# Memory-augmented attention on one core: values and memory reads stay dims-on-partitions until the output product, and the softmax sums are inverted by way of DRAM

## The chip, the core and the metric

The kernel runs on one core of a Trainium2 chip. A core has a matrix engine (TensorE, "PE" in the profile, with its weight loads listed apart as "PEld"), three engines for elementwise work (VectorE "DVE", ScalarE "ACT", GpSimd "POOL") and a sync engine ("SP") whose queue issues most of the DMA transfers here. Each engine takes its instructions in the order of its program and stops at one whose operands aren't ready; whatever stands behind it then waits too. TensorE writes its products into PSUM banks, from which the other engines read.

The metric is the device time of one execution in microseconds (us), lower is better; one execution is also recorded by the hardware profiler, and all profile lines come from such a recording.

## What is computed

Four layers act on x of 2048 tokens by 512 features, 32 heads of 16: a linear attention A, a memory-augmented softmax attention B, and both again. The change is in B:

```python
scale = Dh ** -0.5                       # Dh = 16, L = 512 tokens a segment, N = 4 segments
for s in range(N):
    qs, ks, vs = q[:, :, s], k[:, :, s], v[:, :, s]
    p = _softmax(jnp.einsum("bhqd,bhkd->bhqk", qs, ks) * scale + mask, axis=-1)
    a_dot = jnp.einsum("bhqk,bhkd->bhqd", p, vs)
    pq = phi(qs)                         # phi(t) = t + 1 where t > 0, exp(t) elsewhere
    num = jnp.einsum("bhld,bhde->bhle", pq, M)
    den = jnp.einsum("bhld,bhd->bhl", pq, z)[..., None] + 1e-6
    o = g * (num / den) + (1.0 - g) * a_dot        # g = sigmoid(beta), one number a head
    pk = phi(ks)
    M = M + jnp.einsum("bhld,bhle->bhde", pk, vs)
    z = z + jnp.einsum("bhld->bhd", pk)
# x = x + concat(o) @ wo
```

So each head needs two quotients per token: weighted values over the softmax sum, and the memory's read over its own sum. A sum belongs to a head and a token; it divides 16 numbers.

## The kernel before

**Tiling.** A layer B goes through 4 segments `s` of 512 tokens. The 32 heads are 4 chunks `c` of 8 heads, and a chunk is two head groups of 4 (`hf` 0 and 1), so there are 8 groups `m` a segment and 32 a layer. A group has R = 5 steps. `steps` (L1215) is the loop over all steps `k`. In each it issues, in this order: one logits product with its exponential and masks (`attend`), one step of row maxima for a later group (`maxima`, 9 steps ahead), what was put off from earlier steps, the weighted values of the group before (`weighted`, in steps 0 and 2 of the next group), and then the work named by a table. The tables FIRST, GAPS (the two inner segments), LAST (segment 3 when a layer A follows) and FINAL (segment 3 of the last layer) are written by hand: the cell "4.3 a3 fin out/3" says that in step 3 of group 4 a part of chunk 3's memory work, a `finish` and three quarters of an output product are issued. "q2+" is the Q projection of chunk 2 of the next segment, "~" puts an operation's subtraction off to the next step.

**Order.** Two wrappers fix the order on the engines as it was issued: `held` (L173) chains all matmuls, and `Ordered` (L153) chains the instructions of VectorE, ScalarE, GpSimd and SP each among themselves. That is why nearly all lines of the profile are L163 (`Ordered`'s call), L185 (`mm`) and L189 (`tp`, a transpose on TensorE); what an instruction belongs to is seen by its tiles.

**A group's way.** `attend` (L1084) makes logits with keys on partitions into the one double bank `lg`, and ScalarE's exponential reads them into a `P4` tile of 128 x 1024 (`P` in the profile); a row of the operands carries the negated row maxima, so no subtraction is needed. In every step GpSimd zeroes what the causal mask leaves out (`affine_select`, one or two instructions). `weighted` (L1120) multiplies these tiles with the values: the 4 heads of a group stand on 4 column tiles of 32, so the bank `pv` holds, for each head, 16 dims, the softmax sum (a column of ones stands in the values tile `v`, VW = 17 columns a head) and unused rows, with the 512 tokens along the free axis. ScalarE evicts it to `U`, scaled by 1 - g in the dims' rows (`share`).

**Division.** The sum now lies on one partition and the dims that it divides on 16 others. `finish` (L1147), 8 steps (FINAT) after a group's first, turns `U` with four transposes into a `g` bank, tokens on partitions; there `weigh` (L480) takes the reciprocal of the sums on VectorE, multiplies, and adds on GpSimd into the chunk's tile, `ot` (6 buffers) or `tmp` (2), which the memory's read has filled before.

**Memory.** `memory` (L991) reads for segments 1 to 3: four plain f32 products of 128 x 136 a chunk, tokens on partitions, from the features `phi` of Q and the gated state `kn`; `weigh` divides with 1e-6 added. For segments 0 to 2 it updates: four transposes of phi(K), a ScalarE copy, four accumulating f32 products 128 x 136 with the values, an add to `acc`, and two GpSimd multiplies which make `kn` (block diagonal, dims times the gate). `phi` comes from `proj` (L961): ScalarE takes Exp and Relu of the projection, GpSimd takes the minimum with 1 and adds, 128 x 512 each (tiles `tb` in the profile). I call these two GpSimd operations the feature pair.

**Output.** For a segment's four token tiles `turns` (L1156) transposes the four `ot` tiles back (dims on partitions), splits them into a high and a low half (`turn`, L451: ScalarE copies `oh`, VectorE subtracts `ol`), and asks for the residual rows; `out_proj` (L470) makes the product with `wo` in 12 f32r products of 128 x 512 a token tile and adds the residual. `early`, `end_turn` and `end` do this for the last segment of a layer: the product over three chunks early, the fourth at the end.

**Transfers.** SP's queue is one of the ordered programs. It carries, among others, the weight tiles `wqk` for coming projections (512 KB each, asked for in `proj` once a buffer is free) and the stacking of Q and K parts into the tiles `e` that the logits use (`stack`, 128 KB each, issued for the group three ahead).

Of the kernel before, what the change touches and what calls it, by code (L numbers as in the profile page):

```python
# [15 lines left out]
D = 512  # L16
H = 32
# [10 lines left out]
OT = 6  # L28
TA = 8
OO = 3  # L30
# [23 lines left out]
0.4 v3             | 1.1 max m0 q3/2   | 1.3 fin q3~       | 1.4 t1 k3/1  # L54
2.1 max m1 k3      | 2.3 fin ln~       | 2.4 ln~ ln~
3.3 fin q0+/2      | 3.0 w
3.1 max ln~        | 3.4 q0+~ t2
4.1 max k0+/2 load | 4.3 fin k0+/1     | 4.4 k0+ m2
5.0 n              | 5.3 fin q1+/2 n
5.1 max v0+        | 5.4 q1+~ t3  # L60
6.1 max a0+ v1+    | 6.2 n             | 6.3 a0+ fin k1+/2
6.4 k1+ m3         | 7.0 n             | 7.2 n
7.1 max q2+~       | 7.3 fin v2+/2 n   | 7.4 v2+ t0+
# [6 lines left out]
2.1 max a2 m1 k3~  | 2.3 fin ln out/3  | 2.4 out turn~ ln  # L70
3.1 max ln ln out~ | 3.3 a2 fin q0+/2  | 3.4 q0+~ t2
4.1 max k0+~ a3 turn~ load | 4.3 a3 fin out/3 | 4.4 out~ m2
5.0 n              | 5.3 fin v0+/2 n N
5.1 max q1+~ begin | 5.4 v0+ t3
6.0 N              | 6.1 max a0+ k1+~  | 6.2 n
6.3 a0+ fin v1+/3 N | 6.4 v1+ m3       | 7.0 n N
7.1 max q2+~       | 7.2 n N           | 7.3 fin v2+/2 n N
7.4 v2+ t0+
# [3 lines left out]
0.1 max a1 k2~     | 0.2 n             | 0.3 a1 fin v3/3 n  # L82
1.0 n              | 0.4 v3 turn~      | 1.2 n
1.1 max q3~        | 1.3 fin out/2     | 1.4 out turn~
2.1 max k3~        | 2.3 fin a2 out/2  | 2.4 out a2 turn~
3.1 max ln~ ln~    | 3.3 fin out/2 ln~ | 3.4 out ln~ turn~
4.1 max v/2        | 4.3 fin out/2     | 4.4 out v
5.1 max v/2        | 5.3 fin v         | 5.4 a3 pre
6.1 max v/2        | 6.3 fin v a3      | 6.4 v/2 pt~
7.1 p v pt~        | 7.3 fin v/2 p pt  | 7.4 v p pt  # L90
"""
FINAL = """
0.1 max k2~        | 0.3 fin v3/3      | 0.4 v3 a1
1.1 max a1 q3/2    | 1.3 fin q3~       | 1.4 turn~
2.1 max k3/2       | 2.3 fin k3        | 2.4 out/2
3.1 max a2 out turn~ | 3.3 fin out/2   | 3.4 out~ a2
4.1 max a3 turn~   | 4.3 fin out/2     | 4.4 out/1 a3
5.1 max out turn~  | 5.3 fin out/2     | 5.4 out/1 pre
6.1 max out~       | 6.3 fin           | 6.4 pt~
7.1 p pt~          | 7.3 fin p pt      | 7.4 p pt  # L100
# [7 lines left out]
def interleave_kernel(ctx, tc, x_in, a_wqkv, a_wphi, a_wo, b_wq, b_wk, b_wv, b_wo, b_beta,  # L108
# [86 lines left out]
    bd = cp.tile([P, 27], F32, name="bd")  # L195
    bdA, bdB = bd[:, 0:8], bd[:, 8:16]
# [3 lines left out]
    share = cp.tile([P, 8], F32, name="share")  # L200
    ones = cp.tile([32, P], F32, name="ones")

    def constants():
# [11 lines left out]
        dve.tensor_scalar(share, share, -1.0, bd[:, 24:25], op0=ADD, op1=MUL)  # L215
        dve.tensor_scalar(share, share, 1.0, None, op0=ADD)
        dve.tensor_copy(ones, bd[0:32, 25:26].broadcast_to([32, P]))
# [85 lines left out]
    def prepare():  # L303
# [8 lines left out]
        def rows():  # L312

            while jobs and len(asked) < 5:
                src, kc = jobs.pop(0)
                asked.append(T2("ot", OT))
                sync.dma_start(out=asked[-1], in_=src[kc * P : (kc + 1) * P, :])
            return asked.pop(0)
# [4 lines left out]
        def pieces():  # L323
# [10 lines left out]
            for key in ("awo", "bwv", "bwo"):  # L334
                kept[key] = [dtile((P, NC, D), nm(key)) for _ in range(2)]
                for kc in range(NC):
                    tiles = parts()
                    yield tiles, [k[:, kc, :] for k in kept[key]], tiles[1:]
# [141 lines left out]
    def weigh(out, p, eps, add, eng=pool):  # L480
# [914 lines left out]
```

## Time and profile before

| | us |
|---|---|
| three timed runs | 1470.85, 1476.73, 1477.60 |
| their median | 1476.73 |
| the profiled execution | 1472.48 |
| its span, first to last instruction | 1470.8 |
| TensorE busy | 1425.6 |
| VectorE busy | 1089.4 |
| ScalarE busy | 785.5 |
| GpSimd busy | 651.3 |

The granted TensorE clock of the execution was 0.999 of full speed. A row of the groups view reads: line, engine, operation, tile written <- tiles read, partitions x elements, count | busy us, mean ns of one | idle us of the engine just before them, and what ended most of that idle time. PE rows with a form such as 128\*32 tell the tile of the array (rows \* columns). A row of the stretches view gives a window of the span in us, its length, then for PE, PEld, DVE, ACT, POOL and SP's queue the busy us with the number of instructions, then the granted clock, the busy share of the DMA engines and GB/s. A row of the timeline gives start, length in us, engine, line, operation and tiles. A row of the waits view gives engine and tile waiting <- engine and tile waited for, then total us, how often, and the mean.

### The profile page before, as it was taken

How to read it: one execution, taken by the hardware profiler on the slowest of the kernel's cores; microseconds unless marked ns; L12 is line 12 of the kernel's file. 1: busy time of each engine (PE TensorE's matmuls, PEld its weight loads, DVE VectorE, ACT ScalarE, POOL GpSimd, SP SyncE). 2: the span in 40 equal slices, each digit the busy share in tenths (PEclk: the TensorE clock that was granted, in tenths of full speed). 3: DMA queues.
4: the chain of work that ended last, by engine and by line, in shares of the span. 5: the costliest groups of instructions: out<-in, count | busy, mean ns of one | idle time of the engine just before them, and what ended most of it. 6: DMA issues, size and time to landing. Idle time of an engine off the chain costs nothing.

```text
span 1470.8 us, 32374 instructions
## 1 busy us (share of the span) xinstructions
PE 1425.6 (97%) x11908; PEld 1016.5 (69%) x11908; DVE 1089.4 (74%) x3256; ACT 785.5 (53%) x1178; POOL 651.3 (44%) x1000
## 2 busy tenths in 40 slices
PE   7999999999999999999999999999999999999997
PEld 6877778765666666666578887886566666666564
DVE  4766787778877877878656777867777787777883
ACT  5545345446565565566544434543656655655553
POOL 1668654224443544433324456631444454534331
PEclk9999999999999999999999999999999999999999
DMA  5388275546334434544340105754553353343330
GB/s 189 116 301 280 73 258 172 159 125 178 111 104 135 124 95 113 147 102 135 113 160 28 58 30 183 222 185 116 137 166 104 111 148 102 94 133 101 88 99 37
DMA packets 108781, 195.98 MB, mean 133 GB/s; under 512 B 14416, under 2 KB 27856, under 8 KB 107856
## 3 DMA queue, kind: packets, MB, share of 16 engines
q1 hardware_dynamic: 107472, 193.38, 44.0%
q8 instruction: 96, 1.57, 0.4%
q10 hardware_dynamic: 1152, 0.52, 0.1%
q14 instruction: 61, 0.50, 0.1%
HBM read 101.05 MB, written 39.85 MB: 96 GB/s over the span
## 4 chain that ended last, share of the span: by engine, by line
PE 83%; DVE 11%; ACT 3%; issue 2%; DMA 1%; POOL 1%; SPq 0%; POOLq 0%; ACTq 0%; DVEq 0%
PE g L185 49%; PE pv L185 9%; PE lg L185 9%; PE g L189 6%; PE mx L185 5%; PE my L185 3%; DVE mx L163 2%; DVE es L163 1%; DVE my L163 1%; PE lg L189 1%; ACT P L163 1%; DVE mxs L163 1%; DVE tmp L163 1%; DVE ol L163 1%; DVE rr L163 1%
## 5 line engine op out<-in xcount | busy, mean ns | idle before, releaser
L163 ACT ACTIVATE P<-lg 128x1024 f32<-128x1024 f32 x320 | 329.2, 1029 | 174.9 <-PE lg L185 165.5
L163 POOL TENSOR_SCALAR_AFFINE_SELECT P<-P 128x256 f32<-128x256 f32 (+1 forms) x448 | 191.2, 441 | 450.3 <-ACT P L163 449.5
L163 DVE CUSTOM_DVE_ANT_0 mx<-mx,mask 128x128 f32<-128x128 f32 (+3 forms) x512 | 255.3, 499 | 151.7 <-PE my L185 111.2
L163 DVE CUSTOM_DVE_ANT_0 my<-my,mask 128x128 f32<-128x128 f32 (+3 forms) x512 | 265.8, 519 | 6.5
L185 PE MATMUL g<-hh,wqk 128*128 128x512 f32 x512 | 180.2, 406 | 0.7 <-ACT mt L163 0.7
L185 PE MATMUL lg<-e,e 64*128 64x256 f32 (+2 forms) x1024 | 168.5, 387 | 2.8 <-ACT P L163 2.7
L185 PE MATMUL g<-w,oh 128*128 128x512 f32 x512 | 169.5, 412 | 1.0 <-ACT oh L163 0.7
L185 PE MATMUL pv<-P,v 128*32 128x512 f32 (+3 forms) x2048 | 165.0, 441 | 0.0
L185 PE MATMUL my<-e,e 63*128 63x256 f32 (+2 forms) x512 | 146.5, 346 | 6.7 <-DVE mxs L163 5.6
L185 PEld LDWEIGHTS lg<-e,e 64*128 64x128 f32 x1024 | 81.1, 184 | 98.0 <-issue 52.7
L185 PE MATMUL g<-w,hh 128*128 128x512 f32 x448 | 145.7, 406 | 0.1
L163 DVE DVE_READ_ACCUMULATOR2_ANT mxs<- 128x1 f32 x1024 | 144.7, 141 | 0.0
L185 PE MATMUL mx<-e,e 63*128 63x256 f32 (+2 forms) x512 | 140.3, 329 | 0.3
L185 PEld LDWEIGHTS pv<-P,v 128*32 128x32 f32 x2048 | 53.8, 109 | 100.8 <-issue 91.3
L185 PEld LDWEIGHTS g<-hh,wqk 128*128 128x128 f32 x512 | 96.3, 188 | 22.0 <-ACT mt L163 1.1
L185 PEld LDWEIGHTS g<-w,oh 128*128 128x128 f32 x512 | 88.8, 189 | 23.3 <-issue 2.7
L185 PE MATMUL g<-w,ol 128*128 128x512 f32 x256 | 102.4, 400 | 0.0
L185 PE MATMUL g<-hl,wqk 128*128 128x512 f32 x256 | 100.1, 391 | 0.0
L163 ACT CAST ta<-g 128x512 fp32r<-128x512 f32 x64 | 37.6, 587 | 116.0 <-PE g L185 115.7
L185 PEld LDWEIGHTS my<-e,e 63*128 63x128 f32 x512 | 82.2, 185 | 20.4 <-DVE mxs L163 9.2
L185 PEld LDWEIGHTS mx<-e,e 63*128 63x128 f32 x512 | 90.0, 186 | 5.9 <-DVE mxs L163 1.8
L163 POOL TENSOR_SCALAR tb<-tb 128x512 f32<-128x512 f32 x48 | 71.5, 1489 | 49.8 <-ACT tb L163 49.0
(155 smaller groups left out, 2773.6 us busy)
## 6 DMA issues: line engine op xcount, KB each, us to landing
e<-ta SPq DMA_DIRECT2D x384, 128.0 KB
wqk<-wqk SPq DMA_DIRECT2D x64, 512.0 KB
x<-x SPq DMA_DIRECT2D x48, 256.0 KB
ot<-in SPq DMA_DIRECT2D x28, 256.0 KB
pq<-tb SPq DMA_DIRECT2D x24, 256.0 KB
tb<-pq SPq DMA_DIRECT2D x24, 256.0 KB
x<-xr SPq DMA_DIRECT2D x24, 256.0 KB
xr<-x SPq DMA_DIRECT2D x24, 256.0 KB
```

The lines of the kernel that those rows point to most:

```text
L163: i = f(*a, **k)
L185: return held(nc.tensor.matmul(*a, **k))
L189: return held(nc.tensor.transpose(*a))
```

## The change

In layer B the weighted values are no longer turned to tokens on partitions and back. Dims stay on partitions from `pv` to the output product, and so does the memory's read.

- **Values layout.** `v_tile(paired=True)` interleaves two heads, 34 columns a pair, with ones on both sides, so that group hf 0 has its dims on even rows of `pv`, hf 1 on odd ones; `share` is made to match, and the columns of wv are permuted when they are split.
- **After `weighted`.** `gather` takes every second row of `U` into the chunk's tile `tmp` by an SP transfer (hf 0 to rows 0 to 63, hf 1 to 64 to 127), and the sums' four rows into a DRAM tile `den`. For hf 1, `close` schedules the rest at later steps, counted from k = 5(m + 1) + 2.
- **Inversion.** `invert`: `den` in DRAM to a compact tile `dn` of 128 partitions (k + 2), its reciprocal on VectorE (k + 3), out to DRAM `inv` and from there to DRAM `wide`, 16-fold (k + 4), and as tiles of 128 x 512 into `KN` (values) and `mmq` (memory) (k + 5). For segment 0 only the values' half exists.
- **Closing.** At k + 6 GpSimd multiplies `tmp` by its inverse, and for s > 0 `ot` by its own; at k + 7 it adds the two (s > 0), ScalarE copies the result to `oh`, and GpSimd subtracts for `ol`.
- **Read.** Two products of 64 rows, 68 x 512, into `pv` and a `g` bank; two ScalarE evictions, to `ot` and `mmq`, with 1e-6 added to the sums' rows; SP transfers of the sums to `den` (k + 1) and of the upper numerators into `ot` (k + 2).
- **Update.** `tokens` makes the transposes of phi(K) as before; `update` issues 16 products of 32 columns by 34 on four column tiles instead of four of 136, directly behind `weighted`.
- **Output.** `product` uses `oh`, `ol` as they are; `ask` asks for the residual rows. Chunks 2 and 3 of each layer's last segment keep `finish` with its transposes, then `end_turn`; their memory read alone goes through `invert`.
- **Tables and buffers.** `fin` stays only for the last groups and `turn` is gone; `a`, `m` and `t` cells move, `x` cells ask for residual rows; the scheduled pieces are issued at the end of their step. `ot` has 3 buffers instead of 6, `oh` and `ol` 5 instead of 3.

```diff
-OT = 6
+OT = 3
-OO = 3
+OO = 5
...
 GAPS = """
-0.2 n              | 0.3 a1 fin v3/3 n
-0.1 max a1 k2~     | 0.4 v3 turn~ m0
-1.0 n              | 1.2 n
-1.1 max q3~        | 1.3 fin out/2     | 1.4 out t1 turn~
+0.2 n              | 0.3 v3/3 n
+0.1 max k2~        | 0.4 a1 v3 x0
+1.0 m0 n           | 1.2 n
+1.1 max q3~        | 1.3 out/2         | 1.4 t1 out/1 x1
...
+        def at(self, k, f, *a):
+            self.events.setdefault(k, []).append((f, a))
...
+        def read(self, s, c, k):
+            kn, ph = self.summed(s, c)[1], self.st[s, c]["phi", 0]
+            pn = [PS("pv", PV), PS("g", G)]
+            for a in range(2):
+                mm(pn[a][0:68, :], lhsT=kn[64 * a : 64 * a + 64, :], rhs=ph[64 * a : 64 * a + 64, :],
+                   start=True, stop=True, tile_position=(64 * a, 0))
+            old = self.old[s, c] = T2("ot", OT)
+            upper = T2("mmq", 2)
+            for t, p in zip((old, upper), pn):
+                act.activation(t[0:68, :], p[0:68, :], AF.Identity, bias=bd[0:68, 26:27])
+            def dens():
+                d = self.den(s, c)
+                for a, t in enumerate((upper, old)):
+                    sync.dma_start(out=d[12 - 4 * a : 16 - 4 * a], in_=t[64:68, :])
+            def numerators():
+                sync.dma_start(out=old[64:128, :], in_=upper[0:64, :])
+            self.at(k + 1, dens)
+            self.at(k + 2, numerators)
...
+        def invert(self, s, c, k, parts):
+            lo, hi = 8 * parts[0], 8 * parts[-1] + 8
+            n = (hi - lo) * 4
+            tiles = {}
+            def compact():
+                d = tiles["d"] = T2("dn", 2, shape=(P, 64))
+                sync.dma_start(out=d[:, 0:n], in_=self.den(s, c)[lo:hi].rearrange("h (x i) -> (h x) i", i=n))
+            def flip():
+                dve.reciprocal(tiles["d"][:, 0:n], tiles["d"][:, 0:n])
+            def spread():
+                inv, wide = dtile((hi - lo, D), nm("inv")), dtile((hi - lo, DH, D), nm("wide"))
+                sync.dma_start(out=inv.rearrange("h (x i) -> (h x) i", i=n), in_=tiles["d"][:, 0:n])
+                sync.dma_start(out=wide, in_=inv.unsqueeze(1).broadcast_to([hi - lo, DH, D]))
+                tiles["w"] = wide
+            def load():
+                for i in parts:
+                    t = self.inv[s, c, i] = T2(*(("mmq", 2) if i else ("KN", 1)))
+                    sync.dma_start(out=t, in_=tiles["w"][8 * i - lo : 8 * i - lo + 8].rearrange("h d n -> (h d) n"))
+            for j, f in enumerate((compact, flip, spread, load)):
+                self.at(k + j, f)
+        def gather(self, s, c, hf, U):
+            if hf == 0:
+                self.num[s, c] = T2("tmp", 2)
+            sync.dma_start(out=self.num[s, c][64 * hf : 64 * hf + 64, :], in_=U[1 - hf : P : 2])
+            sync.dma_start(out=self.den(s, c)[4 * hf : 4 * hf + 4], in_=U[31 * hf : P : 32])
...
+        def close(self, s, c, k):
+            self.invert(s, c, k + 2, range(2 if s > 0 else 1))
+            def scaled():
+                o = self.num[s, c]
+                pool.tensor_tensor(out=o, in0=o, in1=self.inv.pop((s, c, 0)), op=MUL)
+                if s > 0:
+                    old = self.old[s, c]
+                    pool.tensor_tensor(out=old, in0=old, in1=self.inv.pop((s, c, 1)), op=MUL)
+            def parts():
+                o = self.num.pop((s, c))
+                if s > 0:
+                    pool.tensor_tensor(out=o, in0=o, in1=self.old.pop((s, c)), op=ADD)
+                hi, lo = self.oT[s, c] = self.outputs(s, c)
+                act.copy(hi, o)
+                pool.tensor_tensor(out=lo, in0=o, in1=hi.bitcast(F32), op=SUB)
+            self.at(k + 6, scaled)
+            self.at(k + 7, parts)
...
+        def update(self, s, c):
+            pk, v = self.pk.pop((s, c)), self.vv[s][0]
+            acc, kn = self.summed(s, c)
+            pm = PS("g", G)[:, 0 : 2 * VW]
+            for t in range(4):
+                for j in range(4):
+                    h = 2 * VW * (4 * c + j % 2) + 1 + j // 2
+                    vh = v[:, t, h : h + 6 * VW].rearrange("p (x e) -> p x e", e=2 * VW)[:, 0:3:2, 0 : 2 * VW : 2]
+                    mm(pm[32 * j : 32 * j + 32, :], lhsT=pk[:, t * P + 32 * j : t * P + 32 * j + 32],
+                       rhs=vh, start=(t == 0), stop=(t == 3), tile_position=(0, 32 * j))
...
             if last:
                 self.pr.pop(m)
                 U = T2("U", 2)
                 act.activation(U, self.pv.pop(m), AF.Identity, scale=share[:, m % 8 : m % 8 + 1])
-                self.U[m] = U
+                k = R * (m + 1) + 2
+                if s == NSEG - 1 and c > 1:
+                    self.U[m] = U
+                else:
+                    self.at(k + (1 if hf else 3), self.gather, s, c, hf, U)
+                    if hf:
+                        self.close(s, c, k)
...
+        def product(self, po, s, t, kcs):
+            yield from mm3(po, lambda a, kc: self.oT[s, kc][a][:, t * P : (t + 1) * P],
+                           lambda b, kc: self.wo[b][:, kc, :], kcs)
...
                 if k % R in (0, 2) and 0 <= k // R - 1 < N:
                     parts.insert(1, [lambda: self.weighted(k // R - 1, k % R == 2)])
+                    parts.insert(2, [lambda s=s, c=c: self.update(s, c) for s, c in memory["m"].get(k, ())])
...
+                put_off[0] = None
+                for f, a in self.events.pop(k, ()):
+                    f(*a)
```

More of the change, by code (lines that the diff above doesn't have):

```diff
@@ L1193, in end @@
                 po = PS("g", G)
-                for _ in mm3(po, lambda a, kc: o[a][:, t * P : (t + 1) * P], lambda b, kc: self.wo[b][:, kc, :],
-                             range(NC - 1, NC)):
+                for _ in self.product(po, s, t, range(NC - 1, NC)):
                     pass
@@ L1222, in steps @@
             norms = [self.norm0]
-            mem = {(s, c): self.memory(s, c) for s in range(NSEG) for c in range(NC)}
             val = [self.values(s) for s in range(NSEG)]
-            outs, turns, proj, part = {}, {}, {}, {}
+            outs, proj, part = {}, {}, {}
             early = self.early()
@@ L1299, in steps @@
                 put_off[0] = None
+                for s, c in memory["a"].get(k, ()):
+                    if s > 0:
+                        self.read(s, c, k)
                 parts = [self.later, self.late]
```

308 lines of the change are left out of this document (165 added, 143 removed).

## The prediction

> **What bounds the kernel now.** I began with the page: the share of each engine, then the chain that ended last.
>
> ```profile
> span 1470.8 us, 32374 instructions
> ...
> PE 1425.6 (97%) x11908; PEld 1016.5 (69%) x11908; DVE 1089.4 (74%) x3256; ACT 785.5 (53%) x1178; POOL 651.3 (44%) x1000
> ...
> PE 83%; DVE 11%; ACT 3%; issue 2%; DMA 1%; POOL 1%; SPq 0%; POOLq 0%; ACTq 0%; DVEq 0%
> ```
>
> The profiled execution took 1472.5 us, of which 1470.8 are its span; the three timed runs have a median of 1476.7, so sums below stand against 1472.5. TensorE is busy for 97% of the span and is 83% of the chain. Next I read busy time by stretch, for an inner segment of the second attention layer and for its last one:
>
> ```profile
> 1135.00:1252.00 117.00, 116.41 (x857) 78.47 (x857) 92.24 (x330) 70.86 (x103) 55.36 (x96) 1.00 0.43 118
> ...
> 1369.00:1464.50 95.50, 90.50 (x665) 54.11 (x663) 65.57 (x227) 49.60 (x64) 29.58 (x60) 0.98 0.26 68
> ```
>
> In the inner segment PE has 0.6 us idle in 117; in the last one 5.0 in 95.5. So PE time that is taken out is worth nearly its length, and anything that makes PE wait costs its full length. The waits tell by what PE can be held:
>
> ```profile
> PEld lg L185 <- ACT P L163: 42.1, 113, 0.8
> ```
>
> There is one bank pair for the logits (`lg`), so the next logits product starts only after ScalarE's exponential has read the last. Call the five steps of a head group 0 to 4; each starts with such a product. Here are the steps 2, 3, 4 of one group and 0, 1 of the next (segment 1, group 5), from the timeline (start, length, engine):
>
> ```profile
> 1205.44 0.33 SPq L163 DMA_DIRECT2D wqk<-wqk  x1
> ...
> 1208.15 1.09 ACT L163 ACTIVATE tb<-g 128x512 f32<-128x512 f32 x2
> ...
> 1208.83 1.49 POOL L163 TENSOR_SCALAR tb<-tb 128x512 f32<-128x512 f32 x1 [0.97 <-ACT tb L163]
> ...
> 1209.12 1.03 ACT L163 ACTIVATE P<-lg 128x1024 f32<-128x1024 f32 x1
> ...
> 1210.21 0.50 PE L185 MATMUL lg<-e,e 64*128 64x256 f32 x4
> ...
> 1210.40 1.29 POOL L163 TENSOR_TENSOR tb<-tb,tb 128x512 f32<-128x512 f32 x1
> ...
> 1210.81 1.03 ACT L163 ACTIVATE P<-lg 128x1024 f32<-128x1024 f32 x1 [0.66 <-PE lg L185]
> ...
> 1211.65 0.77 POOL L163 TENSOR_SCALAR_AFFINE_SELECT P<-P 128x256 f32<-128x256 f32 x2
> ...
> 1212.91 0.50 PE L185 MATMUL lg<-e,e 64*128 64x512 f32 x2
> ...
> 1213.05 0.44 POOL L163 MEMSET v<- 128x128 f32 x2
> 1213.06 0.59 ACT L163 COPY tb<-g 128x512 f32<-128x512 f32 x1
> ...
> 1213.44 0.64 POOL L163 TENSOR_SCALAR_AFFINE_SELECT P<-P 128x512 f32<-128x512 f32 x1
> ...
> 1213.54 1.04 ACT L163 ACTIVATE P<-lg 128x1024 f32<-128x1024 f32 x1
> ...
> 1214.78 0.51 PE L185 MATMUL lg<-e,e 64*128 64x512 f32 x2
> ```
>
> PE's products of step 4 and of the next steps 0 and 1 start at 1210.21, 1212.91 and 1214.78; the exponential of step 0 ends at 1213.54 + 1.04 = 1214.58, 0.2 us before the last of them. A delay of that exponential beyond 0.2 us is PE time lost. GpSimd is meanwhile behind: it does the feature map's two operations (1.49 and 1.29 us, from 1208.83) before the masks of step 3, which end only at 1211.65 + 0.77 = 1212.42.
>
> **What leaves PE.** In instructions: 224 of the 256 transposes of U, the 96 of `ot`, 16 of the 32 of `tmp`; and all of the memory's products, 192 records of reads (`mem,tb`) and 192 of updates (`v,tb`), two records a product.
>
> ```profile
> L185 PE MATMUL pv<-P,v 128*32 128x512 f32 x512 | 69.1, 612 | 0.0
> ...
> L185 PE MATMUL lg<-e,e 64*128 64x512 f32 x256 | 64.6, 501 | 0.7 <-ACT P L163 0.6
> ...
> L189 PE MATMUL g<-ident,U 128*128 128x128 f32 x256 | 41.0, 282 | 1.9 <-ACT U L163 1.6
> ...
> L185 PE MATMUL g<-mem,tb 128*128 128x136 f32 x192 | 32.2, 290 | 0.0
> ...
> L185 PE MATMUL g<-v,tb 128*128 128x136 f32 x192 | 27.2, 281 | 1.0 <-ACT v L163 1.0
> ...
> L189 PE MATMUL g<-ident,ot 128*128 128x128 f32 x96 | 15.8, 274 | 0.6 <-DVE hl L163 0.6
> ...
> L185 PE MATMUL my<-P,v 128*32 128x32 f32 x1024 | 10.9, 199 | 4.9 <-issue 4.9
> ...
> L163 POOL TENSOR_TENSOR st<-st 128x4 f32<-128x4 f32 x56 | 11.5, 206 | 13.1 <-ACT st L163 9.7
> ...
> L189 PE MATMUL g<-ident,tmp 128*128 128x128 f32 x32 | 6.5, 274 | 0.7 <-POOL tmp L163 0.7
> ```
>
> The busy times give the upper price: 41.0 x 224/256 + 15.8 + 6.5/2 + 32.2 + 27.2 = 114 us. They count the drain of each group, which runs beside the next one's work. The lower price is the pitch within a run:
>
> ```profile
> 1152.64 0.87 PE g L189 x8
> ```
>
> ```profile
> 1138.22 0.63 PE L185 MATMUL g<-v,tb 128*128 128x136 f32 x4
> ```
>
> Eight transposes are 0.87 us of the chain, 0.11 each; four records of the update take 0.63 us, of which the last is some 0.28 long (27.2 / 192 is 0.14, its mean 281 ns), so the pitch is 0.12. That is 336 x 0.11 + 384 x 0.12 = 83 us. I take 88: near the pitch, with a little for the starts of groups.
>
> **What comes to PE.** The update becomes 384 products of 34 columns on four column tiles, 768 records. The nearest row is `my<-P,v`, four column tiles and 32 columns: 10.9 us for 1024, so 768 x 34/32 x 10.6 ns = 9 us. Its upper bound, with the 24 groups started alone at 0.28 each and two at a time instead of four, is 24 us. I take 9. The read becomes 48 products of 64 x 512 in plain f32 on two row tiles, 96 records. No row has that form. From above: the f32 record of 512 columns, `pv`, has a mean of 612 ns, 59 us if none runs beside another. From below: four `pv` tiles together need 69.1 us for 512, 0.135 a record; two at a time 0.27, 26 us, and `lg` with 64 rows has 0.25, 24 us. I take 26, the price of records that overlap by two, which is nearest to the two rows of tiles. The Trainium skill (TensorEngine Tiling (Array Packing), Key Properties) says that different tiles can run their products in parallel; the `pv` row agrees, and by it the sum stands. One after another, the records would make the sum 33 us higher.
>
> Not all of it is gained. The exponential of step 3 ended at 1209.12 + 1.03 = 1210.15, just before PE's product at 1210.21: in such groups taking 0.44 us of U's transposes out of step 3 gives nothing. I put 14 of the 56 there, the odd groups of the inner segments, 6 us. So PE gains 88 - 9 - 26 - 6 = 47 us; bounds, 114 - 8 - 24 = 82, and 83 - 24 - 59 - 6, less than nothing (-6).
>
> **What is free.** VectorE loses some 250 small operations and gets 32 reciprocals; it is not the bound, and I count nothing. ScalarE gets two evictions for each of 24 reads, about 0.6 us each (0.59 for the 128 x 512 copy at 1213.06), in step 4, where PE needs 2.7 us (1210.21 to 1212.91) and the exponential ended at 1211.84: 1.1 us of cover, nearly used up; without it each costs what is over. SP issues 332 transfers more, at about 0.33 us (the row at 1205.44). In order, a transfer that waits holds the stacking transfers behind it; these are issued six steps before their use, and the steps shown take 1.9 and 2.7 us, so I count nothing there.
>
> **What comes onto the path: the closing of a chunk.** For 28 of the 32 chunks the sums' inverses go through DRAM and return as a full tile. Then, in GpSimd's order of the changed program, there stand behind the masks of step 3: the multiply of the values, from segment 1 on a second multiply of the memory part, the mask of step 4, the add, and on ScalarE, in front of the next group's exponential, a copy that waits for the add. Two-input operations of 128 x 512 on GpSimd have the row at 1210.40, 1.29 us.
>
> For the group shown: masks end 1212.42; memsets of the next values, 0.44; two multiplies, 2.58, to 1215.44; the mask, 0.64, to 1216.08; the add to 1217.37; the copy, 0.59, to 1217.96; the exponential, 1.04, to 1219.00. That is 4.4 us after 1214.58; less the 0.2 of slack, 4.2 to 4.4 us in which PE waits; I take 4.3. In chunk 2 of a segment six statistics operations (0.21 each) stand before the add instead of the memsets: 5.1. In chunk 3 neither does: 3.9. Mean 4.4. There are 12 closings with the feature pair ahead of them.
>
> The transfers can make it later. In those the inverse is issued behind a load of `wqk`, which waits for PE to be done with step 1:
>
> ```profile
> 1205.44:1206.40 0.96, 0.96 (x10) 0.47 (x14) 0.23 (x1) 0.96 (x2) 0.00 (x0) 1.00 0.02 4
> 1206.40:1209.00 2.60, 2.60 (x30) 1.71 (x23) 2.52 (x8) 2.17 (x4) 0.94 (x3) 1.00 0.62 200
> 1209.00:1210.70 1.70, 1.70 (x14) 1.14 (x12) 1.56 (x8) 1.16 (x2) 1.62 (x2) 1.00 0.00 0
> ```
>
> That load of 512 KB, issued at 1205.44, moved next to nothing for 0.96 us and all of its data by 1209.0, 2.6 us later. Behind it come the inverse on its way out, its 16-fold copy in DRAM (512 KB) and the tile back (256 KB), each waiting for the one before. No row has such trips. From below: the first lands with `wqk`, and the others take their share of the 2.6 us with no start, 2.6 and 1.3; the multiply could begin at 1212.9, when GpSimd is free (1212.42 + 0.44). From above: three trips at 3.6 us, the whole of the load, 1219.8, 6.9 us late. With a start of 0.96 for the last two it would be 1214.8, 1.9 late. I take 1.0, between the first and the third, because the starts may partly overlap; so a closing costs 4.4 + 1.0 = 5.4 us, and twelve 65 us. The Trainium skill (DMA: Bandwidth & Descriptors, Anatomy of one DMA) gives a transfer about 2.0 us fixed and its bytes at 436 GB/s: an estimated 3.2 us for the `wqk` load, and the trace, with 3.6, agrees nearly. By that page the three trips would take an estimated 7.9 us from the end of the issue, the tile would be back at 1213.7, 0.8 late, and the sum would be 2 us lower than mine.
>
> Eight closings of segments 1 to 3 have no feature pair ahead (chunk 0, and chunk 1 of the last):
>
> ```profile
> 1180.09 0.77 POOL L163 TENSOR_SCALAR_AFFINE_SELECT P<-P 128x256 f32<-128x256 f32 x2 [1.22 <-ACT P L163]
> ...
> 1182.22 1.03 ACT L163 ACTIVATE P<-lg 128x1024 f32<-128x1024 f32 x1 [2.19 <-PE lg L185]
> ...
> 1183.35 0.64 POOL L163 TENSOR_SCALAR_AFFINE_SELECT P<-P 128x512 f32<-128x512 f32 x1
> ...
> 1184.94 1.04 ACT L163 ACTIVATE P<-lg 128x1024 f32<-128x1024 f32 x1
> ...
> 1186.19 0.50 PE L185 MATMUL lg<-e,e 64*128 64x512 f32 x2
> ```
>
> Masks end 1180.86; multiplies to 1183.44; the mask to 1184.08; add to 1185.37; copy to 1185.96; exponential to 1187.00, against 1184.94 + 1.04 = 1185.98: 1.0 less 0.2, and more in the short groups of the last segment. I take 1.2 x 8 = 10 us. In segment 0 there is one multiply and no add: in four of eight closings 1212.42 + 1.29 + 0.59 + 1.04 = 1215.34, 0.8 late; 1 x 4 = 4 us; the others fit.
>
> **The sum**: 1472.5 - 47 + 65 + 10 + 4 = 1504.5. I say 1504.
>
> **Rivals.** *PE's gain is the larger, and the kernel is faster.* If the removed groups are worth their busy time (each also ended in an eviction and held a `g` bank) and the reads run in pairs, PE gains 82 - 6 = 76 us. If the tiles are back in time too, the closings cost 12 x 4.4 + 8 x 0.8 + 2 = 61, of which the idle time of the two last segments can take some 10: 1472.5 - 76 + 51 = 1447.5. With no wait at all the 47 alone would give 1425. For it: what leaves PE is certain, and what is waited for is argued. Against it: behind the masks stand 6.6 us of work in one order, from 1212.42 to 1219.00, and the room is 2.2 us, to 1214.58. It decides when all closings together cost less than 69 us at that gain, 3.4 us in each of twenty.
>
> *The transfers set the closing.* At 3.6 us a trip the multiply is 6.9 us late, a closing of the twelve costs 11.3, and the time is 1472.5 - 47 + 136 + 14 = 1575; at half that lateness 1534. It decides when the tile lands later than the 1214.8 of the third count. For it: three trips in a row, and stacking transfers that may share the engines. Against it: after the `wqk` load the DMA share is 0.00.
>
> *Gain and loss cancel*, so that the change doesn't do what it says: closings of 2.4 us in twenty, 47 us against 47, 1472. For it: a copy that is late lets VectorE and GpSimd catch up behind it. Against it: the shortest closing counted, chunk 3, has 3.9.
>
> **Chances.** The forecast 0.50, with a range of its own from 1480 to 1535; the larger gain 0.25, 1425 to 1464; cancelling 0.11, 1465 to 1480; the transfers 0.14, 1535 to 1575. About 0.5% is what a measurement of this kernel can tell from no change. Faster by more: 0.27, the larger gain and a little of the cancelling case; within it 0.11; slower 0.62. The range that leaves out no more than 2 in 10 goes from 1430 to 1550.
>
> **What would show it.** Right: PE's transposes by the page fall by 336 and `g<-mem` and `v,tb` records change as counted; ScalarE's copy `oh<-tmp` appears with idle time ahead of it released by GpSimd, some 4 us in twelve of 28; `lg` loads wait for the exponential by 60 us more than the 42.1. The read's records show at about 0.27 us pitch. Wrong: `oh` without idle time before it (then 1425 to 1447), or GpSimd's multiply idle for a transfer by over 2 us each (then the transfers), or the closing's wait found in VectorE's reciprocal, whose landing I took as in time: behind it stand the row maxima, which PE waits for next.

## The result and the profile after

| | before | after |
|---|---|---|
| median of the timed runs, us | 1476.41 | 1684.07 |
| range of the runs, us | 1470.85 to 1477.60 | 1671.97 to 1692.67 |
| span of the profiled execution, us | 1470.8 | 1690.9 |
| mean granted TensorE clock | 0.999 | 0.921 |

The kernel got slower: ratio 1.1409, 95% interval 1.1328 to 1.149. First the page of the changed kernel, the lines that were shown of before: the span, the engines' busy time, the chain.

```profile
span 1690.9 us, 32954 instructions
...
PE 1444.2 (85%) x12052; PEld 993.8 (59%) x12052; DVE 1021.7 (60%) x3007; ACT 817.4 (48%) x1228; POOL 732.3 (43%) x1066
...
PE 59%; DMA 18%; DVE 8%; POOL 5%; ACT 5%; issue 3%; SPq 2%; ACTq 0%; POOLq 0%; DVEq 0%
```

TensorE is idle for 1690.9 - 1444.2 = 247 us, before for 45; transfers, 1% of the chain before, are 18% of it, some 300 us. But TensorE's busy time did not fall either, and the mean clock says why it could not. The clock record of the trace knows two values, 1.0 and 0.5. After the change it stands at 0.5 for 269 us in 33 spells (2 of these us lie behind the last instruction), with 164 us of TensorE's work in them, which at full clock would have taken 82. So:

| us | before | after | difference |
|---|---|---|---|
| TensorE idle | 45 | 247 | +202 |
| lost to the half clock | 2 | 82 | +80 |
| TensorE work at full clock | 1424 | 1362 | -62 |
| span | 1471 | 1691 | +220 |

The waits view (who waits <- for whom, total us, times, and as the last number the longest, not the mean) names the places:

```profile
PEld lg L185 <- ACT P L163: 212.7, 119, 10.8
ACT oh L163 <- POOL tmp L163: 181.3, 25, 13.7
PE lg L185 <- ACT P L163: 167.7, 52, 10.5
...
POOL tmp L163 <- DMA KN<-wide: 93.1, 19, 12.0
...
DVE dn L163 <- DMA dn<-den: 47.0, 13, 14.4
...
PE mx L185 <- DVE mxs L163: 31.6, 7, 11.8
```

Read from the bottom, the last line aside: VectorE waits for the sums, GpSimd for the tile of inverses, ScalarE's copy `oh` for GpSimd, the logits for the exponential behind that copy. In the last line TensorE waits for VectorE's row maxima, which stand behind the reciprocal of `dn`. Here is one such closing, chunk 1 of segment 1 in the second layer, the place whose steps the prediction showed. From the timeline (start, length, engine), SP's queue, TensorE, GpSimd and ScalarE:

```profile
1350.72 0.34 SPq L163 DMA_DIRECT2D wqk<-wqk  x1
1351.16 0.38 SPq L163 DMA_DIRECT2D inv<-dn  x1
1354.94 0.57 SPq L163 DMA_DIRECT2D wide<-inv  x1
...
1357.55 1.28 PE L185 MATMUL pv<-P,v 128*32 128x512 f32 x16
...
1358.69 0.32 SPq L163 DMA_DIRECT2D KN<-wide  x1
...
1361.39 1.26 POOL L163 TENSOR_TENSOR tmp<-tmp,KN 128x512 f32<-128x512 f32 x1 [4.65 <-DMA KN<-wide]
1362.66 1.26 POOL L163 TENSOR_TENSOR ot<-ot,mmq 128x512 f32<-128x512 f32 x1
1363.88 0.64 POOL L163 TENSOR_SCALAR_AFFINE_SELECT P<-P 128x512 f32<-128x512 f32 x1
1364.48 1.26 POOL L163 TENSOR_TENSOR tmp<-tmp,ot 128x512 f32<-128x512 f32 x1
...
1365.77 0.62 ACT L163 CAST oh<-tmp 128x512 fp32r<-128x512 f32 x1 [8.19 <-POOL tmp L163]
1366.30 1.02 ACT L163 ACTIVATE P<-lg 128x1024 f32<-128x1024 f32 x1
...
1367.37 0.79 PE L185 MATMUL lg<-e,e 64*128 64x512 f32 x2 [8.53 <-ACT P L163]
```

The three trips take 1354.94 - 1351.16 = 3.8, then 3.75 and 2.7 us, 10.2 in all, each issued only when the one before has landed. GpSimd stands still for 4.65 us until the first multiply, then does just the order that the prediction listed; the exponential ends at 1367.32, and TensorE, which stopped at 1357.55 + 1.28 = 1358.83, starts again after 8.53 us. The stretches around it (after the length: PE, PEld, DVE, ACT, POOL busy with their counts, the granted clock, DMA share, GB/s):

```profile
1350.00:1358.50 8.50, 8.06 (x66) 4.75 (x68) 7.20 (x26) 5.84 (x9) 4.56 (x9) 1.00 0.60 185
1358.50:1362.70 4.20, 0.33 (x12) 0.06 (x4) 0.56 (x2) 0.00 (x0) 1.30 (x2) 1.00 0.65 195
1362.70:1367.30 4.60, 0.00 (x0) 0.00 (x0) 0.00 (x0) 1.53 (x2) 3.87 (x4) 0.50 0.60 138
1367.30:1372.95 5.65, 5.58 (x17) 4.39 (x18) 1.85 (x8) 1.19 (x3) 1.20 (x3) 0.50 0.01 1
1372.95:1378.80 5.85, 5.85 (x74) 3.76 (x73) 4.08 (x15) 4.21 (x6) 2.88 (x6) 1.00 0.37 118
```

At 1362.7, 3.9 us into the stall, the clock goes to 0.50, and it stays there for 5.6 us after TensorE has resumed. A projection of this closing shows what that is worth; first the kernel after, then the same products in the kernel before:

```profile
1369.66 1.05 PE L185 MATMUL g<-hh,wqk 128*128 128x512 f32 x2
...
1370.94 1.05 PE L185 MATMUL g<-hh,wqk 128*128 128x512 f32 x2
```

```profile
1202.94 0.63 PE L185 MATMUL g<-hh,wqk 128*128 128x512 f32 x2
...
1203.63 0.63 PE L185 MATMUL g<-hh,wqk 128*128 128x512 f32 x2
```

Between the two rows lie three products: 1.28 us after, 0.69 before.

### The profile page after: what moved, and what is told of

Its sections match the earlier page's. It is cut to its first block, busy times and chain, and to the rows that moved or that the text cites. A ratio compares the mean times of both kernels' runs of the same rounds, so it can differ in the third digit from the quotient of the medians.

```text
span 1690.9 us, 32954 instructions
## 1 busy us (share of the span) xinstructions
PE 1444.2 (85%) x12052; PEld 993.8 (59%) x12052; DVE 1021.7 (60%) x3007; ACT 817.4 (48%) x1228; POOL 732.3 (43%) x1066
## 4 chain that ended last, share of the span: by engine, by line
PE 59%; DMA 18%; DVE 8%; POOL 5%; ACT 5%; issue 3%; SPq 2%; ACTq 0%; POOLq 0%; DVEq 0%
PE g L185 38%; PE lg L185 6%; PE pv L185 5%; DMA inv<-dn 5%; DMA wide<-inv 5%; PE mx L185 3%; PE g L189 3%; POOL tmp L163 2%; SPq L163 2%; ACT P L163 2%; DMA KN<-wide 2%; DMA dn<-den 2%; PE my L185 2%; DVE mx L163 2%; ACT oh L163 1%
## 5 line engine op out<-in xcount | busy, mean ns | idle before, releaser
L185 PE MATMUL lg<-e,e 64*128 64x256 f32 (+2 forms) x1024 | 177.9, 406 | 172.7 <-ACT P L163 167.7
L185 PE MATMUL g<-hh,wqk 128*128 128x512 f32 x512 | 206.8, 462 | 0.7 <-ACT mt L163 0.7
L185 PE MATMUL mx<-e,e 63*128 63x256 f32 (+2 forms) x512 | 153.8, 354 | 31.7 <-DVE mxs L163 31.6
L185 PE MATMUL pv<-P,v 128*32 128x512 f32 (+3 forms) x2048 | 171.5, 455 | 0.0
L185 PE MATMUL my<-e,e 63*128 63x256 f32 (+2 forms) x512 | 154.3, 363 | 8.7 <-DVE mxs L163 7.8
L185 PEld LDWEIGHTS g<-hh,wqk 128*128 128x128 f32 x512 | 114.1, 223 | 31.8 <-issue 5.2
L185 PEld LDWEIGHTS mx<-e,e 63*128 63x128 f32 x512 | 97.7, 200 | 40.8 <-DVE mxs L163 32.5
L185 PE MATMUL g<-hl,wqk 128*128 128x512 f32 x256 | 113.9, 445 | 0.0
L163 ACT CAST oh<-tmp 128x512 fp32r<-128x512 f32 x28 | 17.3, 617 | 197.4 <-POOL tmp L163 181.3
L185 PEld LDWEIGHTS my<-e,e 63*128 63x128 f32 x512 | 92.0, 200 | 24.2 <-DVE mxs L163 13.1
```

The source lines that it names most:

```text
L163: i = f(*a, **k)
L185: return held(nc.tensor.matmul(*a, **k))
```

## The experiments

All numbers in one table; "idle" is span less PE busy of the profiled execution, "half" the time at clock 0.5, "work" PE's busy time less half of that part of it which fell into half clock, "copy" ScalarE's wait for GpSimd at `oh`. The time is the median, the ratio against runs of the kernel before on the same chip.

| run | time | ratio (95%) | idle | half | work | copy |
|---|---|---|---|---|---|---|
| before | 1476 | 1 | 45 | 5 | 1424 | |
| after | 1684.1 | 1.1409 (1.1328 to 1.149) | 247 | 269 | 1362 | 181 |
| e1_later | 1545.0 | 1.0475 (1.0451 to 1.0499) | 132 | 109 | 1368 | 45 |
| e2_copy_later | 1568.0 | 1.0629 (1.0606 to 1.0651) | 143 | 128 | 1370 | 60 |
| e3_no_trips | 1530.8 | 1.0376 (1.0356 to 1.0397) | 121 | 96 | 1368 | 60 |
| e4_spin | 1687.8 | 1.144 (1.1416 to 1.1463) | 121 | 106 | 1518 | 174 |
| e5_apart | 1555.0 | 1.0545 (1.0509 to 1.0582) | 141 | 126 | 1366 | 62 |
| e6_floor | 1469.3 | 0.9963 (0.9943 to 0.9982) | 77 | 34 | 1373 | 6 |
| e7_wqk_behind | 1624.1 | 1.1005 (1.0969 to 1.1041) | 189 | 176 | 1365 | 125 |
| e8_spin_some | 1682.3 | 1.1402 (1.135 to 1.1455) | 189 | 217 | 1416 | 167 |
| e9_all_later | 1501.6 | 1.0164 (1.0114 to 1.0215) | 98 | 74 | 1371 | 11 |
| e10_c3_sooner | 1496.8 | 1.0155 (1.0122 to 1.0187) | 103 | 61 | 1368 | 12 |
| e11_no_wide | 1646.1 | 1.117 (1.1151 to 1.1189) | 208 | 217 | 1364 | 153 |
| e12_no_wide_later | 1460.5 | 0.9905 (0.9888 to 0.9921) | 78 | 43 | 1368 | 12 |

**e1_later: the closing's work two steps later.**

```diff
-            self.at(k + 6, scaled)
-            self.at(k + 7, parts)
+            self.at(k + 8, scaled)
+            self.at(k + 9, parts)
```

> The edit issues the closing's multiplies two steps later (k + 8 instead of k + 6) and its add, copy and subtraction two steps later (k + 9 instead of k + 7). Theory 1 (the trips by way of DRAM set the closing: GpSimd waited 93 us for KN<-wide and 47 us more with the tile as its last operand, of the 181 us that ScalarE's copy waited for GpSimd): two steps are 4 to 5 us, about the lateness of the tile, so the copy's wait falls from 181 to under 70 us, PE's idle time from 247 to under 110, the clock is back near 0.99 and the time is 1420 to 1480. Theory 2 (GpSimd's order, which the prediction priced: two multiplies, a mask and the add ahead of the copy): the order is the same two steps later, so the stall stays above 5 us a closing and the time above 1600.

Theory 2's figure, above 1600, is out; the copy's wait fell as theory 1 said, from 181 to 45 us. The time, 1545, is 65 us above its bound, and the idle time, 132 us, is above the 110 expected. What is left in the trace are gaps of 1.4 to 4.9 us ahead of the logits (the add still stands behind a mask and ahead of the copy) and three of 6.0 to 9.7 us, at the ends of the layers, where VectorE waited for `dn`: 44.7 us in all, nearly as much as the 47.0 before the edit.

**e2_copy_later: only add, copy and subtraction later** (`parts` at k + 9, `scaled` stays at k + 6).

> Only the add, the copy and the subtraction are issued two steps later (k + 9); the multiplies stay at k + 6 and wait for the tile there, with the mask of step 4 behind them. Theory 1 (the late tile is what costs, and ScalarE's copy is the instruction by which TensorE feels it): GpSimd waits as long as before, but its masks are not needed before step 2 of the next group, so most of the stall goes: 1430 to 1500. Rival (a late mask holds the weighted values, which stand ahead of the next logits on TensorE): the wait moves from the exponential to the weighted values, and the time stays above 1560.

1568 is in the rival's range, just above its bound, but its mechanism shows only in small part: by the waits view the weighted values' loads (`PEld pv <- POOL P`) wait 15 us for masks, the logits' loads still 101 us for the exponential. GpSimd waited for the tile as long as before, 97 us against 93, and yet 116 us of the 208 went: more than half of the loss came through the copy ahead of the exponential.

**e3_no_trips: the inversion and its transfers left out, the closing's engine work kept.**

```diff
...
+            for i in parts:
+                self.inv[s, c, i] = lambda: self.wo[0][:, 0, :].bitcast(F32)
+            return
...
-                pool.tensor_tensor(out=o, in0=o, in1=self.inv.pop((s, c, 0)), op=MUL)
+                pool.tensor_tensor(out=o, in0=o, in1=self.inv.pop((s, c, 0))(), op=MUL)
```

> The inverses are not computed and not brought: the transfers dn, inv, wide, KN and mmq and the reciprocal are left out, and GpSimd multiplies with a tile that has long been there (rows of the output weights), so the values are not divided by their sums. All instructions of the closing on GpSimd and ScalarE stay where they are. Theory 1 (trips): what is left is GpSimd's own work, 3.9 to 5.1 us a closing where a feature pair stands ahead and about 1 elsewhere, as in the prediction; the copy's wait falls from 181 to 50 to 80 us, the stalls stay below the 4 us after which the clock was halved, and the time is 1460 to 1510. Theory 2 (the order on GpSimd alone): hardly a change, above 1620.

The copy's wait is in the expected range, 60 us, and the time, 1531, is 21 us above it, since there were still 96 us of half clock, which cost 40 us; the stalls did not stay below 4 us, as was expected. Here is what GpSimd's order alone costs, a closing of chunk 2 (timeline):

```profile
1269.26 1.28 POOL L163 TENSOR_TENSOR tmp<-tmp,w 128x512 f32<-128x512 f32 x1
...
1270.50 1.28 POOL L163 TENSOR_TENSOR ot<-ot,w 128x512 f32<-128x512 f32 x1
...
1271.74 0.63 POOL L163 TENSOR_SCALAR_AFFINE_SELECT P<-P 128x512 f32<-128x512 f32 x1
1272.34 0.48 POOL L163 TENSOR_TENSOR st<-st 128x4 f32<-128x4 f32 x2
...
1273.96 1.26 POOL L163 TENSOR_TENSOR tmp<-tmp,ot 128x512 f32<-128x512 f32 x1
1275.25 0.62 ACT L163 CAST oh<-tmp 128x512 fp32r<-128x512 f32 x1 [4.81 <-POOL tmp L163]
...
1276.84 0.80 PE L185 MATMUL lg<-e,e 64*128 64x512 f32 x2 [5.15 <-ACT P L163]
```

The logits wait 5.15 us; the prediction had 5.1 for chunk 2. All twelve stalls with a feature pair ahead are 3.5 to 5.3 us, 49 us together, and the eight without 1.1 to 1.5, 10 us together. In segment 0 no closing stalls by more than 0.9 us.

**e4_spin and e8_spin_some: idle time filled with products that nobody reads.**

```diff
...
+                if k in self.spin:
+                    idle = PS("mx", 1)
+                    for _ in range(6):
+                        mm(idle, lhsT=ident, rhs=mask, start=True, stop=True)
                 if 0 <= k < R * N:
                     next(at)
```

Six in every closing for e4, five in the closings of chunks 1 to 3 of the inner segments for e8.

> Ahead of the logits product that waits in a closing, six plain f32 products of 128 x 512 into a bank that nobody reads are added, some 5 us of TensorE work that the result doesn't use. Theory 3 (the granted clock of 0.5, seen for 269 us of the changed kernel's span with 164 us of TensorE's work in it, is a price of the idle stretches: 82 us): the idle time is cut short, half clock falls below 120 us, and the kernel gets 30 to 70 us faster although work is added, 1615 to 1655. Rival (the clock falls for another cause, or the added work lengthens the closing as much): 1680 or above.

> As the run with added products, but five of them and only in twelve closings, those of chunks 1 to 3 in the inner segments, where ten of the twelve stalls were 7.6 to 10.8 us. In that run 156 us of work were added, 125 of which filled idle time; the half-clock loss fell from 82 to 43 us. Theory 3 (half clock is a price of idle time): half clock falls by 50 us or more of its 269, and the time to 1645 to 1670. Rival: 1680 or above.

Both missed. In e4 half clock fell by 163 us, as expected, and PE lost 43 us to it instead of 82; but 156 us of work were added where only 126 us of idle time went, so nothing was won. In e8 half clock fell by 52 us, just what was asked, but the loss did not fall at all (85 us against 82), nor did the time. The same closing as above, in e8:

```profile
1354.48 4.56 PE L185 MATMUL mx<-mask,ident 128*128 128x512 f32 x10
...
1364.18 0.80 PE L185 MATMUL lg<-e,e 64*128 64x512 f32 x2 [5.14 <-ACT P L163]
```

The added products start without a gap, but they end long before the exponential does: in eleven of e8's twelve closings 2.1 to 7.2 us of the stall stay idle behind them, and the clock still falls. In twelve of e4's 28 closings no idle time is left behind them, so that what exceeds the stall delays the logits. As a remedy the fill was no use in these two sizes; the price of the half clock stands by the rows above.

**e5_apart: the closing over more steps** (reciprocal and `inv` at k + 4, `wide` at k + 6, the loads at k + 8, multiplies and add at k + 9, copy at k + 10).

> The whole closing is spread over more steps: reciprocal and inv at k + 4, the 16-fold copy at k + 6, the loads at k + 8, both multiplies and the add at k + 9, ScalarE's copy at k + 10 (memory reads of the last segment likewise three steps later). Theory 1 (every wait of the closing is a trip or GpSimd work that stood too near to its reader): VectorE's wait for dn<-den, 47 us in the changed kernel and 45 in the run two steps later, falls below 15, the copy's wait for GpSimd below 25, PE's idle time below 70 us, half clock below 40 us, and the time is 1415 to 1445, under the kernel before. Rival (a fixed cost of the closings is left, as bank or queue contention): above 1470.

Missed, above the rival's 1470. VectorE's wait for `dn` is gone (5.9 us), but GpSimd waited 77 us for a tile that was asked for one step ahead of its use: I had spread the issues and left the last trip, 3.9 us on the mean here from its issue to the multiply, no more room than before.

**e6_floor: no trips (nothing is divided), multiplies and add at k + 9, copy at k + 10.**

> No inversion transfers as in the run without trips (nothing is divided), and GpSimd's multiplies and add at k + 9, ScalarE's copy at k + 10. It measures what TensorE's part of the change is worth without closings that wait: by the trace of the changed kernel TensorE's busy time at full clock is 1362 against 1424 us, 62 less, so 1410 to 1425. If the gain were the prediction's 47 it would be near 1430, if the evictions, gathers and updates cost as much as the transposes saved, above 1460.

1469, above both of the first two figures and in the range of the third, but not for the third's reason: TensorE's work at full clock is 51 us less than before. Idle time is 32 us higher and half clock costs 13 more. Part is this schedule's own: the copy of chunk 3 at k + 10 and the subtraction behind it are late for the output product, four gaps of 2.4 to 2.6 us, each with a spell of half clock behind it. The rest are small waits of the logits for the exponential.

**e7_wqk_behind: the load of `wqk` one step later in SP's queue, nothing else.**

```diff
...
-                dma(w, wqk[m][:, c])
...
+                    self.at(self.now + 1, dma, w, wqk[m][:, c])
...
```

> Only the order of SP's queue is changed: each load of wqk is issued one step later, so that in a closing it stands behind the inverse, its 16-fold copy and the loads of the tiles. Theory 1a (the inverse's first trip is long, 3.6 to 7 us against 1.5 us where no such load is ahead, because the load is under way): the first trip falls to some 2 us in the sixteen or so closings concerned, each stall by about 2 us, and the time by 25 to 60 us, to 1625 to 1660. Rival (the load takes its time from a later trip instead): 1675 or above.

As theory 1a had it, to 1 us beyond its range: 60 us for the order of one transfer. The time from the issue of `inv` to that of `wide` fell from 3.5 to 2.7 us on the mean of 28 closings, in its median from 3.7 to 2.0.

**e9_all_later and e10_c3_sooner: later work, `wqk` behind, the add with the multiplies.**

```diff
...
-                self.invert(s, c, k + 3, range(1, 2))
+                self.invert(s, c, k + 5, range(1, 2))
...
-                self.at(k + 7, scaled)
+                self.at(k + 12, scaled)
...
-            for j, f in enumerate((compact, flip, spread, load)):
+            for j, f in ((0, compact), (2, flip), (2, spread), (3, load)):
...
-            self.at(k + 6, scaled)
-            self.at(k + 7, parts)
+            self.at(k + 8, scaled)
+            self.at(k + 10, parts)
```

> All that the runs so far point to, together: the load of wqk behind the closing's trips; the reciprocal one step later with inv and the 16-fold copy still at k + 4 (reciprocal at k + 4) and the loads at k + 5; multiplies and add at k + 8; ScalarE's copy at k + 10; the subtraction of chunk 3 on VectorE; the memory reads' inversion in the last segment started two steps later, so that it doesn't stand between the other closing's trips on SP. Theory 1: the copy's wait for GpSimd falls below 25 us, VectorE's for dn below 15, PE's idle time below 75 us, half clock below 40, and the time is 1425 to 1455, under the kernel before. Rival (the in-order queue of SP hands the trips' waits on to stacking or residual transfers): above 1480.

> As e9_all_later, but chunk 3's copy at k + 9 and its subtraction on GpSimd: the output product that reads it stands in the step after k + 10, and in the run without trips TensorE lost 2.4 us and a half-clock window there in each of five segments. Theory: the same or up to 15 us faster than e9_all_later; if the copy then waits for the add, up to 15 us slower.

In e9 the wait came as expected for the copy (11 us), not for `dn` (23 us), nor did idle time (98 us) and half clock (74 us), and the time is in the rival's range. e10 is 5 us faster, as its theory had it, but that is less than the spread of the runs. The largest gap left in each, 10.2 and 8.5 us, stands where a layer B ends: there SP issues loads for the next layer (`w<-awv`) ahead of one closing's `inv`, and VectorE's reciprocal waits for the next chunk's `dn`, which stands behind that closing's trips.

**e11_no_wide and e12_no_wide_later: one trip less, the tiles read straight from `inv`,** in the changed kernel as it is and in e10.

```diff
...
-                sync.dma_start(out=wide, in_=inv.unsqueeze(1).broadcast_to([hi - lo, DH, D]))
-                tiles["w"] = wide
+                tiles["w"] = inv
...
-                    sync.dma_start(out=t, in_=tiles["w"][8 * i - lo : 8 * i - lo + 8].rearrange("h d n -> (h d) n"))
+                    sync.dma_start(out=t, in_=tiles["w"][8 * i - lo : 8 * i - lo + 8].unsqueeze(1).broadcast_to([8, DH, D]))
```

> The changed kernel with one trip less and nothing else: the tiles KN and mmq are read straight from inv, each row 16 times, and the 16-fold copy in DRAM is left out. By the changed kernel's rows the trip over wide takes about 4 us a closing, in 28 closings. Theory 1 (trips): idle time falls by 28 x 3 to 4 us = 85 to 110, half clock by 60 us or more, and the time from 1684 to 1545 to 1590. Rival (the closing is set by GpSimd's order, or the reads with 16-fold rows are as slow as the copy they replace): above 1640.

> As e10_c3_sooner (everything later, wqk behind) and without the 16-fold copy. Theory 1: the rest of e10's stalls that stem from SP's order and the trips goes, the copy's wait is below 10 us, idle time below 70, and the time is 1440 to 1475, at or under the kernel before. Rival (what is left in e10 has other causes): 1485 or above.

e11 is 38 us faster than the changed kernel, but its 1646 is in the rival's range, and the second half of the rival is what the trace shows: the trips' sum fell by 2.0 us a closing, not 4: the tile's own trip takes 4.3 us on the mean instead of 2.8, the first one 4.0 instead of 3.5. e12 is inside its range, although the copy's wait (12 us) and the idle time (78 us) are a little above what was expected. Of the versions that divide it is the one that beats both kernels, by 0.95% against the kernel before; its four runs, 1458 to 1466, lie clear of that kernel's seven, 1470 to 1475. Its page and its waits:

```profile
PE 1386.6 (95%) x12052; PEld 956.0 (65%) x12052; DVE 1022.5 (70%) x3007; ACT 813.4 (56%) x1228; POOL 731.0 (50%) x1066
...
PE 72%; DVE 10%; ACT 6%; DMA 5%; issue 4%; POOL 1%; SPq 1%; ACTq 0%; DVEq 0%; POOLq 0%
```

```profile
PEld lg L185 <- ACT P L163: 70.1, 125, 2.8
...
DVE dn L163 <- DMA dn<-den: 17.5, 4, 9.7
...
POOL tmp L163 <- DMA KN<-inv: 12.9, 3, 8.5
...
ACT oh L163 <- POOL tmp L163: 11.6, 4, 7.6
```

All four waits are far below those of the changed kernel; the logits' wait, 70 us, is still above the 42 of the kernel before.

## Why the prediction was wrong, point by point

**What leaves and what comes to TensorE: right in size.** 88 - 9 - 26 = 53 us were forecast; with the trips out of the way the work is 51 to 56 us less (e6, e3, e12). The rows that were missing (groups view):

```profile
L185 PE MATMUL pv<-tb,mem 64*68 64x512 f32 x48 | 24.5, 588 | 0.0
L185 PE MATMUL g<-tb,mem 64*68 64x512 f32 x48 | 24.5, 588 | 0.0
L185 PE MATMUL g<-v,tb 128*32 128x34 f32 x768 | 11.6, 200 | 0.0
```

```profile
1379.44 0.59 PE L185 MATMUL pv<-tb,mem 64*68 64x512 f32 x1
...
1379.87 0.59 PE L185 MATMUL pv<-tb,mem 64*68 64x512 f32 x1
```

The records of the two row tiles run beside each other, 0.43 us a pair: 48 x 0.43 = 21 us for the reads, where I took 26 and feared 59. The update is 11.6 us busy, where I took 9.

**What of that is gained: too high.** I took off 6 us where the exponential sets the pace. In e12's profiled execution the work is 56 us less, idle time 33 us higher, and half clock costs 16 us more, so the span is only 6 us shorter (13 us by the medians). So even with closings that hardly wait most of the gain goes where something else ends last. Of the cause only a part is shown: the logits' longer wait for the exponential and the gaps at the layers' ends.

**GpSimd's order at a closing: right.** 65 us less the 12 for lateness, and 10 and 4 more, are 67. In the run without trips the closings' stalls are 49 + 10 = 59 us, single ones 3.5 to 5.3 and 1.1 to 1.5 us against 3.9 to 5.1 and 1.0 (1.2 as charged); the 4 us for segment 0 did not come.

**The transfers' lateness: the term that failed.** "I take 1.0, between the first and the third, because the starts may partly overlap." They don't overlap: SP's queue issues each trip when the one before has landed, and the three took 3.48 + 4.04 + 2.84 = 10.4 us on the mean, beside my upper bound of 3 x 3.6. By the Trainium skill (DMA: Bandwidth & Descriptors, Anatomy of one DMA), whose fit is for transfers that GpSimd issues, it was an estimated 7.9; these, which SP issues, show 10.4. I also charged it to twelve closings only. The eight of segment 0, which have no second multiply and for which I had 4 us, stalled TensorE for 41 us together, the first in each layer for 9.8 and 8.4; without the trips none of them does by more than 0.9. Instead of 12 us the trips cost 247 - 121 = 126 us of idle time, by the run without them, and 82 - 40 = 42 us of half clock. 60 us of the kernel's time hang on where `wqk` stands, which the prediction saw and priced by a landing "with `wqk`".

**The reciprocal, "whose landing I took as in time":** it was not, 47 us in 13 waits. Four of them, at the ends of the two layers B, stopped TensorE ahead of the row maxima for 5.6 to 11.8 us, 29 us together. That sentence named the right sign, and I gave it no price.

**What was in no term: the half clock.** 80 us, more than a third of the difference. It is why the measured time lies above even the rival of the transfers, whose mechanism is the one that came true: 1575 + 80 = 1655 as an estimate, and the waits for `dn` are not in it. The Trainium skill (TensorE: Matmul & The Clock Gate, Part 1) says that the clock of TensorE falls to half after an idle window of about 3.4 us and returns after a busy one. This case agrees in the length: 32 of the 33 spells last a multiple of 3.41 us, and half clock sets in 3.9 us after the stop in the closing shown. It differs in that the clock also falls when TensorE was idle for only part of the time (figures in the last section). The run without trips shows what that adds to the stalls that were forecast: each of its twelve stalls of 3.5 to 5.3 us has a spell of half clock at it, which costs 1.7 to 3.4 us, 29 us together. The prediction has no such term.

## What to carry to other kernels

A round trip through DRAM is counted per trip, in full, and so is everything that stands ahead of it in the queue that issues it; three dependent trips took 10 us here. The reader of such a result belongs behind work that may wait, not ahead of the operation by which the busiest engine is fed: the same instructions two steps later took 139 us off. Price a stall of the matrix engine of 3.5 us or more at its length and half of the work that then runs at half clock: 3.3 to 6.3 us of time, 5 on the mean, behind the stalls of the logits in the changed kernel.

## What the runs showed of the hardware

The granted clock changes on a fixed raster. Cut into stretches of 3.41 us, the changed kernel's trace has no fall to 0.5 without a stretch before it in which TensorE was busy for 70% or less, mostly under 40%. That is no threshold: stretches busy for 52 to 69% also stand in this trace with no fall behind them. Each spell but the last, which the end of the trace cuts, ends with a stretch that was busy for 82% or more, nearly all for 96% or more. Filling a stall in part need not help: in e8 the idle time was 58 us shorter and the half clock's loss no smaller. And a read that fetches each row of 2 KB from DRAM sixteen times took 4.3 us, where the same tile from an expanded copy took 2.8; each from issue to the multiply; the cause of that was not tried.
